# Weight chunks queued ahead of attention loads, a three-step path for the first block's weights, and six offsets for an operand pair

## Chip, cores and metric

The kernel runs on one NeuronCore of one Trainium2 chip. The metric is the device time of one execution in microseconds (us), the median of repeated runs. Engines are named as the profile names them: PE is TensorE, PEld its weight loads, DVE is VectorE, ACT is ScalarE, POOL is GpSimd, SP is SyncE, whose queue issues all of this kernel's DMAs.

## The reference, cut to what matters

Three stages run in a row over 4608 tokens of width 512.

```
# attention in chunks of 64, 8 batches x 8 heads x 576 x 64 (q, k, v are float32)
scores = q_c @ k_c.T / sqrt(64);  attn = softmax(scores);  x = attn @ v_c
x = x.transpose(0, 2, 1, 3).reshape(4608, 512)
# first MoE: w_in 512 x 2048, w_out 2048 x 512 (float64)
h = x @ w_in
g = h * clip(h + 3, 0, 6) / 6
x = g @ w_out
# second MoE: w_in 512 x 1024, w_out 1024 x 512 (float64), g_ln
h = x @ w_in
solu = h * softmax(h)
out = layernorm(solu) * g_ln @ w_out
```

The weights are float64 in device memory, so every chunk of them is converted to float32 on the core before it is used.

## The kernel before, in words

**Stages.** 36 attention units of 128 tokens make 9 blocks of 512 tokens. The first MoE runs block by block; the attention units of the next block are computed inside the current block, in `slot(b, f)`. Each block loops over 16 chunks `f` of the hidden width. Per chunk, `moe_h` (L267) does 12 matmuls with the stationary chunk `wi[f]`, and `moe_o` (L292) does 12 with `wo[f]`. Twelve, because each operand is split into a high and a low part and three of the four products are kept. `moe_o` is called one chunk late: PE's order is h(f), out(f-1), h(f+1), out(f). The second MoE takes 36 tiles of 128 tokens: `h2(t)`, 24 matmuls with the stationary operand `x_hi`/`x_lo`, and three tiles later `out_t`, 24 matmuls with the stationary operand `l_hi`/`l_lo` and the moving operand `wi`.

**A weight chunk's way in the first block.** `fetch` (L127) brings 512 KB of float64 words by an SP DMA. `rescale` (L139) is one ACT pass over the high words. `convert` (L144) is DVE work into an int32 tile `s` (4 buffers in rotation): one AND (L152) and two shift-or operations (L157) per chunk. With two chunks in one call the order is AND, AND and then four shift-ors, alternating. `split_w` (L170) takes the next chunk from the queue `ready`: an ACT cast to the high part (L73) and a POOL subtraction for the low part (L74), both reading `s`. Chunks of `w_in` are called i0 to i15 here, those of `w_out` o0 to o15.

**The activation's way.** After h(f): ACT relu into `t` (L278), DVE product with the clip (L282), ACT cast to `g_hi` (L73), and in the first and the last block a POOL subtraction to `g_lo` (L74).

**Order.** The schedule is manual: each engine executes its instructions in the order in which the code issues them, and waits in that order. In the first block, an iteration f of the code issues h(f) with its relu, one split (chunk i f+2), the activation's three steps, `convert` of o f and i f+3, out(f-1), the attention slot, rescales for o f+1 and i f+4, and one split (chunk o f). The slot puts eight small exponentials per unit on ACT where f is a multiple of 4 (L214), and a normalising product on DVE (L228).

**Buffers.** Tiles lie one behind the other in their pools. All tiles allocated ahead of the second MoE's pools have a length that is a multiple of 512 bytes, apart from a few small ones at the very start, so that `x_hi`, `x_lo`, `g_hi`, `g_lo`, `wi` and `wo` all begin at the same place within 512 bytes. The second MoE's pool `b2` begins there too; it holds ten [128, 1] tiles of 32 bytes each among its large ones, and pool `b3` with `l_hi` and `l_lo` (three buffers each) comes behind it. So `l_hi` and `l_lo` begin 320 bytes further within 512 bytes than `wi`.

**PSUM.** `ps_att`, `ps_h` have two banks each, `ps_acc` four, for the sums of `moe_o`. Ahead of the first block the attention units 0 to 3 use banks of `ps_att` and `ps_h`.

Of the kernel before, what the change touches and what calls it, by code (L numbers as in the profile page):

```python
# [8 lines left out]
F32 = mybir.dt.float32  # L9
F32R = mybir.dt.float32r  # L10
# [6 lines left out]
P = 128  # L17
# [4 lines left out]
def tile_kernel(  # L22
# [59 lines left out]
    def wo_slot(f, dtype):  # L82
        return wap.tile([P, 2, DM], dtype, tag=f"wo{f}", name=f"wo{f}")
# [43 lines left out]
    def fetch(kind, f):  # L127
        src = {"i": w_in, "o": w_out, "2": w_in2}[kind]
        if kind == "2" and f >= KD * NS:
            src = w_out2[f - KD * NS]  # L130
        else:
            src = src[f]
        raw = SLOTS[kind](f, F32).rearrange("p w n -> p (w n)").rearrange("p (n w) -> p n w", w=2)
        raws[kind, f] = raw
        nc.sync.dma_start(
            out=raw.bitcast(I32), in_=src.bitcast(I32).rearrange("p (n w) -> p n w", w=2)
        )

    def rescale(*key):  # L139
        if key in raws:  # L140
            r = raws[key][:, :, 1]
            nc.scalar.activation(out=r, in_=r, func=AF.Copy, scale=2.0**-112)  # L142
# [48 lines left out]
    def attn_scores(u, ps=att_psum, pt=None):  # L191
        scv = scores(u, ps)
        mx = ap2.tile([P, H], F32, tag="mx", name="mx")
        nc.vector.tensor_reduce(out=mx, in_=scv, axis=AX.X, op=ALU.max)
        pt = att_tile(ap2, "p") if pt is None else pt
        nc.vector.tensor_sub(
            out=pt, in0=scv, in1=mx[:, :, None].to_broadcast([P, H, D])
        )
        nc.scalar.activation(out=pt, in_=pt, func=AF.Exp, scale=0.125)
        p_t[u] = pt  # L200
# [111 lines left out]
                nc.sync.dma_start(out=x2d[b, :, dc], in_=xo)  # L312


    kbs, qps, vs = [kbd], [], []
    for i in range(3):
        kbs.append(wo_slot(NF - 1 - i, F32).rearrange("p c (h k) -> p c h k", h=H))
    for i in range(3, 6):
        qps.append(wo_slot(NF - 1 - i, F32).rearrange("p c (h k) -> p c h k", h=H))
    vs = wo_slot(NF - 7, F32).rearrange("p c (h k) -> p c h k", h=H)  # L320

    load_qk(0)
    load_qk(1, qps[0][:, 0], diagonal(kbs[1], nc.gpsimd))
# [5 lines left out]
    fetch("i", 1)  # L329
    load_v(2, vs[:, 0])  # L330
    load_v(3, vs[:, 1])
    fetch("o", 0)
    fetch("i", 2)
    fetch("o", 1)
    nc.sync.dma_start(out=g_sb, in_=g_ln)
    make_identity(nc, ident)
    diagonal(pbd, nc.gpsimd)
    nc.gpsimd.memset(three, 3.0)
    xs = new_x()
    attn_scores(0)  # L340
    attn_scores(1)
    load_qk(4)
    attn_norm(0, nc.gpsimd)
    attn_scores(2, h_psum, qps[0][:, 1])
    attn_transpose(0, pbd, h_psum)
    rescale("i", 0)
    attn_norm(1)
    attn_scores(3, h_psum, qps[1][:, 1])
    attn_transpose(1, kbs[1])
    attn_norm(2)  # L350
    attn_pv(0, pbd, *xs)
    load_v(4)
    attn_transpose(2, kbs[2], h_psum)
    attn_norm(3)
    convert(("i", 0))
    attn_pv(1, kbs[1], *xs)
    load_v(5)
    rescale("i", 1)
    attn_transpose(3, kbs[3], h_psum)
    split_w(1)  # L360
    attn_pv(2, kbs[2], *xs)
    convert(("i", 1))
    attn_pv(3, kbs[3], *xs)
    rescale("i", 2)
    split_w(1)
    attn_scores_act(4)
    load_qk(5)
    for f in range(2, NF):
        if f < NF - 7:
            fetch("o", f)  # L370
        if f + 1 < NF:
            fetch("i", f + 1)
    for f in range(NF - 7, NF):
        fetch("o", f)
    convert(("i", 2))
    rescale("o", 0)
    rescale("i", 3)
    x2, xr2 = {}, {}

    def fetch_x2(c):  # L380
# [47 lines left out]
    for b in range(NB):  # L428
        first, last = b == 0, b == NB - 1
        if not last:  # L430
            xn[b + 1] = new_x()
        for f in range(NF):
            h = moe_h(f, *xn[b])
            if first:
                split_w(1)
            pend.append((b, f, moe_g(*h, nc.gpsimd if first or last else nc.vector)))
            if f % 4 == 3:
                slot(b, f)
            if first:
                convert(("o", f), ("i", f + 3))  # L440
            if len(pend) > 1:
                moe_o(*pend.pop(0))
            if f % 4 != 3:
                slot(b, f)
            if first:
                rescale("o", f + 1)
                rescale("i", f + 4)
            split_w(1 if first else 2)
            if last:
                fetch("2", f)  # L450
                rescale("2", f - 1)
# [13 lines left out]


    b2 = ctx.enter_context(tc.tile_pool(name="b2", bufs=2, reuse_waits="tile"))
    b3 = ctx.enter_context(tc.tile_pool(name="b3", bufs=3, reuse_waits="tile"))
    ps_2 = ctx.enter_context(tc.tile_pool(name="ps_2", bufs=3, space=PSUM, reuse_waits="tile"))
    ps_o = ctx.enter_context(tc.tile_pool(name="ps_o", bufs=2, space=PSUM, reuse_waits="tile"))  # L470

# [2 lines left out]
    def h2(t):  # L474
        x_hi, x_lo = x2[t // UPB]
        o = (t % UPB) * P
        hp = ps_2.tile([P, FF2], F32, tag="h2", name="hp2")
        for s in range(NS):
            n = 0
            for kk in range(KD):  # L480
                for a, w in ((x_hi, 0), (x_hi, 1), (x_lo, 0)):
                    nc.tensor.matmul(  # L482
                        hp[:, s * DM : (s + 1) * DM], a[:, kk, o : o + P], wi[kk * NS + s][:, w],
                        start=(n == 0), stop=(n == 3 * KD - 1),
                    )
                    n += 1
        nmx = b2.tile([P, 1], F32, tag="nmx", name="nmx")
        nc.vector.tensor_reduce(out=nmx, in_=hp, axis=AX.X, op=ALU.max, negate=True)  # L488
        e = b2.tile([P, FF2], F32, tag="e", name="e")
        r = b2.tile([P, 1], F32, tag="r", name="r")  # L490
        nc.scalar.activation(out=e, in_=hp, func=AF.Exp, bias=nmx, accum_out=r)  # L491
        nc.vector.tensor_scalar_add(out=r, in0=r, scalar1=1e-9)
        nc.vector.reciprocal(out=r, in_=r)
        mu = b2.tile([P, 1], F32, tag="mu", name="mu")
        nc.vector.scalar_tensor_tensor(
            out=e, in0=e, scalar=r, in1=hp, op0=ALU.mult, op1=ALU.mult, accum_out=mu
        )
        nc.vector.tensor_scalar_mul(out=mu, in0=mu, scalar1=1.0 / FF2)
        d = b2.tile([P, FF2], F32, tag="d", name="d")
        nc.vector.tensor_scalar_sub(out=d, in0=e, scalar1=mu)  # L500
        d_t[t] = d
# [16 lines left out]
    def chain_square(t):  # L518
        d = d_t.pop(t)
        junk = b2.tile([P, FF2], F32, tag="junk", name="junk", bufs=1)  # L520
        va = b2.tile([P, 1], F32, tag="va", name="va")
        nc.scalar.activation(out=junk, in_=d, func=AF.Square, accum_out=va)
        va_t[t] = va

    def chain_rstd(t):
        va = va_t.pop(t)
        nc.vector.tensor_scalar(
            out=va, in0=va, scalar1=1.0 / FF2, scalar2=1e-6, op0=ALU.mult, op1=ALU.add
        )
        y = b3.tile([P, 1], F32, tag="y", name="y", bufs=4)  # L530
        yi = y.bitcast(I32)
        nc.vector.tensor_single_scalar(
            out=yi, in_=va.bitcast(I32), scalar=1, op=ALU.logical_shift_right
        )
        nc.vector.tensor_scalar(
            out=yi, in0=yi, scalar1=-1.0, scalar2=float(RSQRT_SEED), op0=ALU.mult, op1=ALU.add
        )
        tt = b2.tile([P, 1], F32, tag="tt", name="tt")
        for _ in range(3):
            nc.gpsimd.tensor_mul(out=tt, in0=y, in1=y)  # L540
            nc.gpsimd.tensor_mul(out=tt, in0=tt, in1=va)
            nc.gpsimd.tensor_scalar(
                out=tt, in0=tt, scalar1=-0.5, scalar2=1.5, op0=ALU.mult, op1=ALU.add
            )
            nc.gpsimd.tensor_mul(out=y, in0=y, in1=tt)
        rs_t[t] = y

    def split_l(t):
        turn_moves(t, (0, 1), nc.scalar.copy)
        m = m_t.pop(t)[0].rearrange("p a (f j) -> p f a j", j=32)  # L550
        l_hi = b3.tile([P, NF2, P], F32R, tag="l_hi", name="l_hi")
        l_lo = b3.tile([P, NF2, P], F32R, tag="l_lo", name="l_lo")
        hv, lv = [l.rearrange("p f (a j) -> p f a j", j=32) for l in (l_hi, l_lo)]
        split(hv, lv, m, nc.gpsimd)
        l_t[t] = (l_hi, l_lo)
# [90 lines left out]
```

## Time and profile before

| | us |
|---|---|
| median of 3 runs | 1311.71 (1311.7 to 1312.77) |
| the profiled execution, its own time | 1311.98 |
| the profiled execution, span from first to last instruction | 1310.0 |
| PE busy in the span | 1277.4 (98%) |
| PEld, DVE, ACT, POOL busy | 1041.7, 794.0, 581.8, 298.5 |
| chain that ended last: PE 89%, issue 3%, POOL 3%, DVE 2% | |

The page gives each engine's busy time, the chain of work that ended last, and the costliest groups of instructions. A matmul record is longer than the distance to the next one, since matmuls overlap, so rates are read from the distance between starts. A stretch is given in us from the start of the span.

### The profile page before, as it was taken

Reading aid. Unit: us, or ns where it says so; the run is one execution under the profiler, and the core shown is the slowest. Engines: PE = TensorE matmul, PEld = TensorE weight load, DVE = VectorE, ACT = ScalarE, POOL = GpSimd, SP = SyncE. Lnnn points to the kernel's source line nnn. Section 1 sums busy time; section 2 is a strip of 40 time slices with the busy share of each in tenths; the row PEclk is TensorE's granted clock in tenths of the full one; section 3 lists DMA queues with packets and bytes.
Section 4 is the critical chain, followed back from the end, with each engine's and each line's share of the span. In section 5 each row is a group of like instructions: output and inputs, shape, how many; then the busy total and the mean of one; then the engine's idle time right before and its main releaser. Section 6 shows DMA issues by size and latency. Waiting matters only on the chain.

```text
span 1310.0 us, 17877 instructions
## 1 busy us (share of the span) xinstructions
PE 1277.4 (98%) x6368; PEld 1041.7 (80%) x6368; DVE 794.0 (61%) x1556; ACT 581.8 (44%) x1106; POOL 298.5 (23%) x562
## 2 busy tenths in 40 slices
PE   6699999999999999999999999999999999999998
PEld 5566788888888888888888888888888888888887
DVE  6788655655655655656555555469766555555542
ACT  4566422222322222222322222445687666666665
POOL 2465200000000000000000000355355444444444
PEclk9899999999999999999999999999999999999999
DMA  7910110110110210200200200444132221222111
GB/s 236 409 62 25 57 49 25 57 49 25 58 47 25 77 29 25 81 25 25 81 25 28 78 25 1 129 129 129 28 94 82 80 81 49 81 81 73 57 49 57
DMA packets 52649, 92.41 MB, mean 71 GB/s; under 512 B 9552, under 2 KB 18768, under 8 KB 52560
## 3 DMA queue, kind: packets, MB, share of 16 engines
q1 hardware_dynamic: 52560, 91.27, 21.8%
q8 instruction: 50, 0.82, 0.2%
q14 instruction: 39, 0.32, 0.1%
HBM read 62.92 MB, written 18.87 MB: 62 GB/s over the span
## 4 chain that ended last, share of the span: by engine, by line
PE 89%; issue 3%; POOL 3%; DVE 2%; DMA 1%; ACT 1%; SPq 1%; POOLq 0%; ACTq 0%; DVEq 0%
PE acc L298 27%; PE hp L272 26%; PE po L564 15%; PE hp L482 15%; PE att L261 2%; PE att L186 2%; POOL g_lo L74 1%; POOL wo L74 1%; DMA wi<-in_moe_w_in 1%; DVE s L157 1%; POOL wi L74 1%; DVE s L152 1%; SPq L112 0%; DVE x_lo L74 0%; DVE t L282 0%
## 5 line engine op out<-in xcount | busy, mean ns | idle before, releaser
L298 PE MATMUL acc<-g_hi,wo 128*128 128x512 f32 x1152 | 295.0, 397 | 16.1 <-ACT wo L73 14.2
L272 PE MATMUL hp<-x_hi,wi 128*128 128x512 f32 x1152 | 285.1, 390 | 0.0
L298 PEld LDWEIGHTS acc<-g_hi,wo 128*128 128x128 f32 x1152 | 213.1, 189 | 73.1 <-ACT wo L73 18.9
L278 ACT ACTIVATE t<-hp,three 128x512 f32<-128x512 f32 x144 | 99.0, 687 | 372.6 <-PE hp L272 372.2
L272 PEld LDWEIGHTS hp<-x_hi,wi 128*128 128x128 f32 x1152 | 215.9, 188 | 44.9 <-ACT wi L142 0.2
L282 DVE SCALAR_TENSOR_TENSOR t<-t,hp 128x512 f32<-128x512 f32 x144 | 99.1, 688 | 234.4 <-ACT t L278 234.4
L74 POOL TENSOR_TENSOR g_lo<-t,g_hi 128x512 fp32r<-128x512 f32 x32 | 45.8, 1431 | 715.1 <-PE acc L298 672.5
L482 PE MATMUL hp<-wi,x_hi 128*128 128x512 f32 x576 | 177.8, 390 | 0.0
L298 PE MATMUL acc<-g_lo,wo 128*128 128x512 f32 x576 | 154.4, 390 | 0.0
L272 PE MATMUL hp<-x_lo,wi 128*128 128x512 f32 x576 | 153.9, 389 | 0.0
L564 PE MATMUL po<-wi,l_hi 128*128 128x512 f32 x576 | 140.2, 396 | 0.0
L251 DVE STREAM_TRANSPOSE pbd<-p 32x128 f32<-32x128 f32 x448 | 135.3, 302 | 5.7
L73 ACT CAST g_hi<-t 128x512 fp32r<-128x512 f32 x144 | 89.3, 620 | 107.9 <-DVE t L282 107.9
L564 PEld LDWEIGHTS po<-wi,l_hi 128*128 128x128 f32 x576 | 108.3, 188 | 25.6
L482 PEld LDWEIGHTS hp<-wi,x_hi 128*128 128x128 f32 x576 | 108.2, 188 | 23.5
L298 PEld LDWEIGHTS acc<-g_lo,wo 128*128 128x128 f32 x576 | 108.6, 189 | 22.9
L74 POOL TENSOR_TENSOR l_lo<-m,l_hi 128x1024 fp32r<-128x1024 f32 x36 | 86.6, 2406 | 174.1 <-ACT l_hi L73 152.0
L272 PEld LDWEIGHTS hp<-x_lo,wi 128*128 128x128 f32 x576 | 108.1, 188 | 22.5
L74 DVE TENSOR_TENSOR g_lo<-t,g_hi 128x512 fp32r<-128x512 f32 x112 | 77.6, 693 | 76.8 <-ACT g_hi L73 76.8
L516 ACT COPY m<-tr 32x256 f32<-32x256 f32 x288 | 115.8, 402 | 2.9
L482 PE MATMUL hp<-wi,x_lo 128*128 128x512 f32 x288 | 112.4, 390 | 0.0
L491 ACT ACTIVATE e<-hp,nmx 128x1024 f32<-128x1024 f32 x36 | 40.2, 1116 | 111.3 <-DVE nmx L488 111.3
(91 smaller groups left out, 1299.7 us busy)
## 6 DMA issues: line engine op xcount, KB each, us to landing
wi<-in_moe_w_in SPq DMA_DIRECT2D x24, 512.0 KB, 7.3
x2d<-xo SPq DMA_DIRECT2D x36, 256.0 KB, 2.8
xo<-x2d SPq DMA_DIRECT2D x36, 256.0 KB, 4.3
m<-tr SPq DMA_DIRECT2D x288, 32.0 KB, 1.8
out<-ob SPq DMA_DIRECT2D x36, 256.0 KB, 2.2
v<-in_v SPq DMA_DIRECT2D x34, 256.0 KB, 2.6
q<-in_q SPq DMA_DIRECT2D x33, 256.0 KB, 3.5
kbd<-in_k SPq DMA_DIRECT2D x66, 128.0 KB, 3.5
```

Source lines behind the costliest of these rows:

```text
L73: nc.scalar.copy(out=hi, in_=src)
L74: (eng or nc.vector).tensor_sub(out=lo, in0=src, in1=hi.bitcast(F32))
L186: nc.tensor.matmul(sc[r0 : r0 + D, h // 2], qt[:, h], kt[:, :, h], start=True, stop=True)
L251: nc.vector.transpose(out=pb[o : o + 32, s // 2, c, s % 2], in_=pv[s * 32 : s * 32 + 32, c, e],)
L272: nc.tensor.matmul(hp, wi[f][:, a, kk * P : (kk + 1) * P], b[:, kk], start=(n == 0), stop=(n == 3 * KD - 1),)
L278: nc.scalar.activation(out=t, in_=hp, func=AF.Relu, bias=three[:])
L282: nc.vector.scalar_tensor_tensor(out=t, in0=t, scalar=6.0, in1=hp, op0=ALU.min, op1=ALU.mult)
L298: nc.tensor.matmul(acc[dc], wo[f][:, w, dc * P : (dc + 1) * P], g[i], start=(f == 0 and n == 0), stop=(f == NF - 1 and n == 2),)
L482: nc.tensor.matmul(hp[:, s * DM : (s + 1) * DM], a[:, kk, o : o + P], wi[kk * NS + s][:, w], start=(n == 0), stop=(n == 3 * KD - 1),)
L491: nc.scalar.activation(out=e, in_=hp, func=AF.Exp, bias=nmx, accum_out=r)
L516: move(out=m[b * 32 : b * 32 + 32, a], in_=tr[a * 32 : a * 32 + 32, b])
L564: nc.tensor.matmul(po, a[:, f], wi[KD * NS + f][:, w], start=(n == 0), stop=(n == 3 * NF2 - 1),)
```

## The change

- **Fetch order.** i2, i3, i4 and o2 are fetched earlier, ahead of the loads of unit 4 or right behind them, and i5, o3, i6, o4 ahead of the load of unit 5, which waits for the scores of unit 4. In the rest, `fetch("i", f + 2)` stands ahead of `fetch("o", f)`. The small load of `g_ln` moves behind unit 5's.
- **Attention units 0 to 3** write their scores into the four accumulator banks, their transposes into `ps_att`, and their products into `ps_h`. The conversion of i0 is issued ahead of the normalisation of unit 2.
- **First block.** `convert` is issued ahead of the activation's steps, and for o f+1 instead of o f (i f+3 as before). An iteration has two splits as before: the first is now chunk o f (issued between `convert` and the activation's steps), the second is i f+2 (issued behind the slot). Rescales are for o f+2 and i f+4. So a chunk is converted in one iteration, split in the next and used by PE in a later one.
- **Second MoE.** The small tiles move into a pool `bs` behind `b3`. Each of the three buffers of `l_hi` and `l_lo` becomes a tile of its own, 512 bytes longer than its contents, which begin 0, 16 and 64 elements (`l_hi`) or 8, 32 and 112 elements (`l_lo`) behind the tile's start.

```diff
+    def acc_psum(i):
+        return lambda: ps_acc.tile([P, DM], F32, tag=f"acc{i}", name=f"acc{i}")
...
     load_v(3, vs[:, 1])
+    fetch("i", 2)
     fetch("o", 0)
-    fetch("i", 2)
+    fetch("i", 3)
     fetch("o", 1)
-    nc.sync.dma_start(out=g_sb, in_=g_ln)
...
-    attn_scores(0)
-    attn_scores(1)
+    attn_scores(0, acc_psum(0))
+    attn_scores(1, acc_psum(1))
     load_qk(4)
+    fetch("i", 4)
+    fetch("o", 2)
     attn_norm(0, nc.gpsimd)
-    attn_scores(2, h_psum, qps[0][:, 1])
-    attn_transpose(0, pbd, h_psum)
+    attn_scores(2, acc_psum(2), qps[0][:, 1])
+    attn_transpose(0, pbd)
     rescale("i", 0)
     attn_norm(1)
-    attn_scores(3, h_psum, qps[1][:, 1])
+    attn_scores(3, acc_psum(3), qps[1][:, 1])
     attn_transpose(1, kbs[1])
+    convert(("i", 0))
     attn_norm(2)
-    attn_pv(0, pbd, *xs)
+    attn_pv(0, pbd, *xs, h_psum)
+    attn_transpose(2, kbs[2])
+    rescale("i", 1)
+    attn_norm(3)
+    attn_pv(1, kbs[1], *xs, h_psum)
+    split_w(1)
     load_v(4)
-    attn_transpose(2, kbs[2], h_psum)
-    attn_norm(3)
-    convert(("i", 0))
-    attn_pv(1, kbs[1], *xs)
     load_v(5)
-    rescale("i", 1)
-    attn_transpose(3, kbs[3], h_psum)
-    split_w(1)
-    attn_pv(2, kbs[2], *xs)
+    fetch("i", 5)
+    fetch("o", 3)
+    fetch("i", 6)
+    fetch("o", 4)
+    attn_transpose(3, kbs[3])
     convert(("i", 1))
-    attn_pv(3, kbs[3], *xs)
+    attn_pv(2, kbs[2], *xs, h_psum)
     rescale("i", 2)
+    attn_pv(3, kbs[3], *xs, h_psum)
     split_w(1)
     attn_scores_act(4)
     load_qk(5)
...
-    convert(("i", 2))
     rescale("o", 0)
+    convert(("i", 2), ("o", 0))
     rescale("i", 3)
+    rescale("o", 1)
...
             h = moe_h(f, *xn[b])
             if first:
+                convert(("o", f + 1), ("i", f + 3))
                 split_w(1)
             pend.append((b, f, moe_g(*h, nc.gpsimd if first or last else nc.vector)))
             if f % 4 == 3:
                 slot(b, f)
-            if first:
-                convert(("o", f), ("i", f + 3))
             if len(pend) > 1:
                 moe_o(*pend.pop(0))
             if f % 4 != 3:
                 slot(b, f)
             if first:
-                rescale("o", f + 1)
+                split_w(1)
+                rescale("o", f + 2)
                 rescale("i", f + 4)
-            split_w(1 if first else 2)
+            else:
+                split_w(2)
...
-    b3 = ctx.enter_context(tc.tile_pool(name="b3", bufs=3, reuse_waits="tile"))
+    b3 = ctx.enter_context(tc.tile_pool(name="b3", bufs=1, reuse_waits="tile"))
+    bs = ctx.enter_context(tc.tile_pool(name="bs", bufs=2, reuse_waits="tile"))
...
+    L_AT = {"l_hi": (0, 16, 64), "l_lo": (8, 32, 112)}
+
+    def l_tile(name, i):
+        o = L_AT[name][i]
+        l = b3.tile([P, FF2 + P], F32R, tag=f"{name}{i}", name=f"{name}{i}")
+        return l[:, o : o + FF2].rearrange("p (f t) -> p f t", t=P)
...
-        l_hi = b3.tile([P, NF2, P], F32R, tag="l_hi", name="l_hi")
-        l_lo = b3.tile([P, NF2, P], F32R, tag="l_lo", name="l_lo")
+        l_hi, l_lo = l_tile("l_hi", t % 3), l_tile("l_lo", t % 3)
```

## Rows read from the trace of the kernel before

**Rows 1.** Busy time by stretch: PE, PEld, DVE, ACT, POOL, PEclk, DMA share, GB/s.

```profile
25.00:30.00 5.00, 4.31 (x42) 3.55 (x43) 4.07 (x8) 3.38 (x6) 1.97 (x2) 1.00 0.15 55
30.00:43.00 13.00, 3.54 (x16) 2.61 (x14) 8.29 (x12) 6.38 (x24) 3.27 (x3) 0.78 0.98 373
43.00:152.00 109.00, 102.38 (x515) 77.87 (x516) 87.04 (x122) 64.35 (x147) 59.77 (x44) 0.98 0.32 118
```

**Rows 2.** PE's waits from 28 to 152 us: total us, times, longest.

```profile
PE acc L298 <- ACT wo L73: 14.2, 7, 9.6
```

**Rows 3.** Timeline of PE, first block: the start of out(0), out(1), out(12), out(15).

```profile
43.12 3.78 PE L298 MATMUL acc<-g_hi,wo 128*128 128x512 f32 x8 [9.58 <-ACT wo L73]
...
50.70 1.19 PE L298 MATMUL acc<-g_hi,wo 128*128 128x512 f32 x4
...
128.97 1.20 PE L298 MATMUL acc<-g_hi,wo 128*128 128x512 f32 x4 [0.73 <-ACT wo L73]
...
149.54 1.98 PE L298 MATMUL acc<-g_hi,wo 128*128 128x512 f32 x8
```

**Rows 4.** Timeline of POOL in one iteration of the first block.

```profile
65.12 1.29 POOL L74 TENSOR_TENSOR wo<-s,wo 128x512 fp32r<-128x512 f32 x1 [3.50 <-ACT wo L73]
66.36 1.29 POOL L74 TENSOR_TENSOR wi<-s,wi 128x512 fp32r<-128x512 f32 x1
67.61 1.48 POOL L74 TENSOR_TENSOR g_lo<-t,g_hi 128x512 fp32r<-128x512 f32 x1
```

**Rows 5.** Timeline of DVE at the same place.

```profile
61.76 0.43 DVE L152 TENSOR_SCALAR s<-wo 128x512 int32<-128x512 int32 x1
62.10 0.42 DVE L152 TENSOR_SCALAR s<-wi 128x512 int32<-128x512 int32 x1
...
65.79 0.69 DVE L282 SCALAR_TENSOR_TENSOR t<-t,hp 128x512 f32<-128x512 f32 x1 [0.86 <-ACT t L278]
66.40 1.54 DVE L152 TENSOR_SCALAR s<-wo 128x512 int32<-128x512 int32 x1
67.86 1.52 DVE L152 TENSOR_SCALAR s<-wi 128x512 int32<-128x512 int32 x1
69.29 0.68 DVE L157 SCALAR_TENSOR_TENSOR s<-wo,s 128x512 int32<-128x512 int32 x1
69.90 0.68 DVE L157 SCALAR_TENSOR_TENSOR s<-wi,s 128x512 int32<-128x512 int32 x1
```

**Rows 6.** Timeline of all engines: a POOL operation issued between DVE's.

```profile
46.31 1.58 POOL L74 TENSOR_TENSOR g_lo<-t,g_hi 128x512 fp32r<-128x512 f32 x1 [0.18 <-ACT g_hi L73]
46.33 0.41 DVE L152 TENSOR_SCALAR s<-wi 128x512 int32<-128x512 int32 x1
46.66 1.77 DVE L157 SCALAR_TENSOR_TENSOR s<-wo,s 128x512 int32<-128x512 int32 x1
```

**Rows 7.** Timeline of ACT: a rescale, and one slot's eight exponentials, first and behind.

```profile
35.80 0.65 ACT L142 ACTIVATE wi<-wi 128x512 f32<-128x512 f32 x1 [5.99 <-DMA wi<-in_moe_w_in]
...
95.04 0.62 ACT L73 CAST g_hi<-t 128x512 fp32r<-128x512 f32 x1 [0.25 <-DVE t L282]
95.56 0.31 ACT L214 ACTIVATE p<-att,mx 128x64 f32<-128x64 f32 x1
...
97.89 0.72 ACT L142 ACTIVATE wo<-wo 128x512 f32<-128x512 f32 x1
```

**Rows 8.** Timeline of PE, a later block: 24 matmuls stand between these starts.

```profile
317.43 1.98 PE L298 MATMUL acc<-g_hi,wo 128*128 128x512 f32 x8
...
322.87 1.98 PE L298 MATMUL acc<-g_hi,wo 128*128 128x512 f32 x8
```

**Rows 9.** Timeline of PE, second MoE: 24 matmuls of `out_t`, then 24 of `h2`.

```profile
1106.48 3.90 PE L564 MATMUL po<-wi,l_hi 128*128 128x512 f32 x16
...
1112.08 0.62 PE L482 MATMUL hp<-wi,x_hi 128*128 128x512 f32 x2
...
1117.55 3.90 PE L564 MATMUL po<-wi,l_hi 128*128 128x512 f32 x16
```

More of the change, by code (lines that the diff above doesn't have):

```diff
@@ L312, in moe_o @@
                 nc.sync.dma_start(out=x2d[b, :, dc], in_=xo)
-    kbs, qps, vs = [kbd], [], []
+    kbs, qps = [kbd], []
     for i in range(3):
@@ L367, in tile_kernel @@
     load_qk(5)
[L368 to L372, printed above, removed]
+    nc.sync.dma_start(out=g_sb, in_=g_ln)
+    for f in range(5, NF - 7):
+        fetch("i", f + 2)
+        fetch("o", f)
     for f in range(NF - 7, NF):
+        if f + 2 < NF:
+            fetch("i", f + 2)
         fetch("o", f)
-    convert(("i", 2))
     rescale("o", 0)
+    convert(("i", 2), ("o", 0))
     rescale("i", 3)
+    rescale("o", 1)
     x2, xr2 = {}, {}
@@ L486, in h2 @@
                     n += 1
-        nmx = b2.tile([P, 1], F32, tag="nmx", name="nmx")
+        nmx = bs.tile([P, 1], F32, tag="nmx", name="nmx")
         nc.vector.tensor_reduce(out=nmx, in_=hp, axis=AX.X, op=ALU.max, negate=True)
         e = b2.tile([P, FF2], F32, tag="e", name="e")
-        r = b2.tile([P, 1], F32, tag="r", name="r")
+        r = bs.tile([P, 1], F32, tag="r", name="r")
         nc.scalar.activation(out=e, in_=hp, func=AF.Exp, bias=nmx, accum_out=r)
@@ L493, in h2 @@
         nc.vector.reciprocal(out=r, in_=r)
-        mu = b2.tile([P, 1], F32, tag="mu", name="mu")
+        mu = bs.tile([P, 1], F32, tag="mu", name="mu")
         nc.vector.scalar_tensor_tensor(
@@ L520, in chain_square @@
         junk = b2.tile([P, FF2], F32, tag="junk", name="junk", bufs=1)
-        va = b2.tile([P, 1], F32, tag="va", name="va")
+        va = bs.tile([P, 1], F32, tag="va", name="va")
         nc.scalar.activation(out=junk, in_=d, func=AF.Square, accum_out=va)
@@ L529, in chain_rstd @@
         )
-        y = b3.tile([P, 1], F32, tag="y", name="y", bufs=4)
+        y = bs.tile([P, 1], F32, tag="y", name="y", bufs=4)
         yi = y.bitcast(I32)
@@ L537, in chain_rstd @@
         )
-        tt = b2.tile([P, 1], F32, tag="tt", name="tt")
+        tt = bs.tile([P, 1], F32, tag="tt", name="tt")
         for _ in range(3):
```

## The prediction

> **What bounds the kernel now.** I read the busy times by stretch first, then PE's waits, then the timelines of single engines. Behind 152 us PE has no wait worth a term, so the loss sits ahead of that. There the stretches show three things. From 25 to 30 us the DMA engines are nearly idle (share 0.15): SP's queue stands at the load of unit 5. From 30 to 43 us PE is busy 3.5 of 13 us. From 43 to 152 us PE looks busy, but POOL and DVE together take 59.8 + 87.0 of 109 us [rows 1]. PE's only large wait there is for the casts of `wo`, 14.2 us, 9.6 of them ahead of out(0) [rows 2, 3]. The reader should see how out(0) comes to be late: o0 is converted in one call with i3, and i3's rescale waits for its DMA until 35.80 [rows 7].
>
> From out(1) to out(12) the block takes (128.97 - 50.70) / 11 = 7.12 us an iteration [rows 3]. PE's own need is 5.44 us for 24 matmuls [rows 8]. What fills the rest? A free AND takes 0.42 us; with a POOL subtraction running it takes 1.52, and it ends 0.3 us behind POOL [rows 4, 5]. So a conversion and a POOL subtraction exclude each other. POOL gets in between two DVE instructions that follow without a gap: issued at 46.31, it runs behind the AND that ends at 46.74, until 47.89 (1.15 us), and the shift-or issued at 46.66 ends only at 48.43 [rows 6]. The product with the clip, which reads PSUM, isn't held: 0.69 us with POOL busy. One iteration holds six conversions (to the start of what follows: 2 x 0.34 + 4 x 0.60 = 3.08 us) and three subtractions (1.25 apart). Before, the three subtractions run one behind the other from 65.12 to 69.09, while relu, product and `g_hi` are made beside them, and then the shift-ors run. Exclusive work stands nearly without a gap, and that is the 7.12.
>
> **The change part by part.**
>
> *Fetch order.* The DMA gap goes, and i3 is there before its rescale is due. PE gains only what no other wait takes over, so I price it inside the start-up below.
>
> *Start-up.* The conversion of i0 (0.42 + 2 x 0.7 = 1.8 us) moves ahead of unit 2's normalisation on DVE, in the attention chain; part of it fills a DVE gap, so h(0) starts about 1 us later, near 28.8. The extra banks free scores, transposes and products of each other, but the chain runs through DVE and ACT, so I price them at nothing; the DVE work above hides them, and without that cover they could be worth what h(0) loses, 1 us. Then DVE does i2 with o0 from about 30.2 to 33.3, and o1 with i3 behind it, with i2's subtraction in between: to 37.5. Only then comes the product of chunk 0, because `convert` is now issued ahead of it. `g_hi` is ready at 38.8, eight exponentials follow on ACT (95.56 to 97.89: 2.3 us [rows 7]), and o0's cast, which now stands behind the slot, ends near 41.8. So out(0) starts at 41.8 instead of 43.12. The stall that i3's DMA caused goes to DVE and ACT: 1.3 us gained, not 9.6. The unit's product and o0's subtraction then put the AND of i4 at 43.85.
>
> *Three steps.* PE and ACT no longer wait for a conversion of the same iteration. But a new ring closes. `convert` in iteration f takes two `s` tiles. With four in rotation, i f+3 takes that of i f+1, which POOL reads in the second split of iteration f-1. POOL does that behind `g_lo` of f-1, which needs the product of f-1, which stands on DVE behind the conversion of f-1. Before, i f+3 took the tile of i f+1 as well, but POOL had split that ahead of `g_lo` of f-1. Round the ring, from the AND of i f+3: 0.34 + 4 x 0.60 to the start of the product; o f's subtraction gets in between, 1.15 (rows 6); product 0.69, `g_hi` 0.62, `g_lo` 1.25, subtraction of i f+2 1.25, and 0.25 that I allow for three hand-overs. Sum: 7.95 us, against 7.12. During product and `g_hi` neither side has exclusive work, and that 1.3 us is the loss.
>
> The slot adds to the ring, since the second split now stands behind it on ACT. At f = 4, 8, 12 the exponentials hold i f+2's cast for 2.3 us, of which `g_lo` hides little, and unit product and subtraction exclude each other: +2.25. At f = 2, 6, 10 two copies of 0.58 each: +0.5. At f = 3, 7, 11 one cast and the unit's DVE work: +0.25. Out(1) can start when `g_hi` of 1 is ready: 43.85 + 0.34 + 2.40 + 1.15 + 0.69 + 0.62 = 49.1 (50.70 before). Eleven iterations later: 49.1 + 11 x 7.95 + 3 x 0.5 + 3 x 0.25 + 2 x 2.25 = 143.3 for out(12), where it was 128.97. The last two conversions have no `w_in` partner (three operations, 1.0 us less): 7.95 - 1.0 + 2.25 = 9.2 and 6.9 us, to 159.4 for out(14); behind it h and one more round put out(15) at 165 instead of 149.54. From there PE sets the pace as before. Part: +15.5 us.
>
> Bounds. If o f's subtraction fell into the gap of 1.3 us, the ring would be 6.8 us and the part about +2.5; rows 6 speak for the other place. If a second AND or the rescales fell into the ring (0.34 each), +20.
>
> *Six offsets.* In the first MoE 24 matmuls take 5.44 us, 226.6 ns each [rows 8]; in `out_t` (1112.08 - 1106.48) / 24 = 233.3; in `h2` 5.47 us in all [rows 9]. The first two differ in where the stationary operand lies against the moving one: at the same place within 512 bytes, and 320 bytes off. After, the six tiles lie 0, 64, 256 (`l_hi`) and 32, 128, 448 bytes (`l_lo`) off. If the place is the cause, the tile at 0 gains 12 x 16 x 6.7 ns = 1.3 us for certain; all six would gain 864 x 6.7 ns = 5.8, and `h2` 1.0 more. Nothing in the trace says what the other five do; as a bound they cost as much again as 320 bytes does, 672 x 6.7 ns = 4.5, less the 1.3. I take -3.0, ends -6.8 and +3.2: the tile at 0 and about a third of the rest. The Trainium skill speaks against any gain (SBUF — State Buffer, "Who interferes with whom"): TensorE has two read ports of its own, one for moving data and one for weights, and never waits on anyone. By that rule the offsets are worth nothing and the sum is 1327.5; the trace, with 233.3 against 226.6 ns for the same shape, doesn't fit that the place is indifferent, though it doesn't prove it.
>
> *Nothing else.* Moving the small tiles changes no operation; blocks 1 to 8 keep their order, as the `else` branch is the old one.
>
> Sum against the profiled execution, 1311.98 (2 us over its span, 0.3 over the median of the runs): + 15.5 - 3.0 = 1324.5; I say 1324.
>
> **Rivals.** *The ring doesn't bind* (faster). Place: the AND of i f+3. If its `s` tile is free before `g_lo` of f-1 has run, DVE converts beside the activation chain. Then only the exclusive work counts, 2.74 + 3 x 1.15 = 6.2 us an iteration, more than PE's 5.44: out(15) near 41.8 + 15 x 6.2 + 2 = 137, -12.5, with the offsets 1296.5. It decides where that AND starts: within 2 us of the product before it, or behind i f+1's subtraction. For it speaks that PE's 14.2 us of waits are for the very casts that move [rows 2]; against it the order of POOL's queue. Chance 0.13.
>
> *POOL's o split in the gap*: ring 6.8, block +2.5, in all 1311.5, no change. Chance 0.13.
>
> *PE's clock falls.* PE would be idle some 2.5 us in each ring and 5 at the slots with exponentials; from 30 to 43 us the granted clock was 0.78 on average, and out(0)'s first eight matmuls took 3.78 us against 1.98 later [rows 1, 3]. If that spread, PE would need 5.44 x 3.78 / 1.98 = 10.4 us a ring at the lower level (1.2 GHz): over four or five rings some 11 us more, 1335. Against it: in the block before, with 1.7 us an iteration beyond the 24 matmuls, 0.98 was granted. Chance 0.06.
>
> **How the numbers follow.** The forecast has 0.68: its own range, from the ring's bounds and those of the offsets, is 1315 to 1333. The range that should hold 8 of 10 reaches down to the rival without change: 1307 to 1333. A run of this kernel can tell 0.2% (2.6 us). Faster: 0.13 and a quarter of the third case, 0.16. Same: half of that, 0.07. Slower: 0.77.
>
> **What the profile after would show.** Right: out(0) near 42, out(1) near 49; from there starts of out(f) about 8 us apart and 10 behind each slot with exponentials; the AND of i f+3 starting just behind POOL's `wi` subtraction; DVE idle for over 1 us behind each product; out(15) near 165; PE waiting for `g_hi` or `g_lo`, not for `wo`. `out_t` at 226.6 ns for tiles t with t mod 3 = 0 at least. Wrong: starts of out(f) under 7 us apart, or an AND that runs beside `g_hi`; or `out_t` at 233 throughout.

## The result and the profile after

The changed kernel takes 1324.7 us (median of 4 runs, 1324.05 to 1325.35), the kernel before 1312.2 beside it. The ratio is 1.0095 (95% interval 1.0078 to 1.0113): slower by 0.95%. The span of the profiled execution grew by 12.5 us, from 1310.0 to 1322.5.

The stretches of [rows 1], in the same columns, with the last one reaching to the end of the slow part:

```profile
25.00:30.00 5.00, 4.35 (x53) 3.97 (x54) 4.92 (x7) 4.55 (x10) 2.29 (x2) 0.88 1.03 398
30.00:43.00 13.00, 7.01 (x26) 5.18 (x25) 9.84 (x20) 7.62 (x26) 7.41 (x5) 0.88 1.04 367
43.00:168.00 125.00, 103.98 (x512) 82.17 (x511) 83.03 (x115) 60.73 (x143) 59.72 (x43) 0.93 0.24 86
```

The fetch order did its part: from 25 to 30 us the DMA share is 1.03 instead of 0.15, and from 30 to 43 us PE is busy 7.01 us instead of 3.5. The loss is in the last row: 512 PE instructions are spread over 125 us. Here is what PE waited for in the first block (line, total, times, longest), beside [rows 2], without two waits of 0.6 us:

```profile
PE acc L298 <- ACT g_hi L73: 13.2, 6, 3.3
PE att L261 <- ACT pbd L239: 7.2, 4, 2.9
PE acc L298 <- ACT wo L73: 6.0, 1, 6.0
```

Before, the waits were for `wo`. Now out(f) finds its weight chunk late once, at out(0), and from then on the activation is late (`g_hi`), and with it the attention slot. The starts of some out(f) on PE, beside [rows 3]:

```profile
40.64 3.88 PE L298 MATMUL acc<-g_hi,wo 128*128 128x512 f32 x8 [5.99 <-ACT wo L73]
49.06 1.98 PE L298 MATMUL acc<-g_hi,wo 128*128 128x512 f32 x8
...
141.84 3.49 PE L298 MATMUL acc<-g_hi,wo 128*128 128x512 f32 x8 [2.39 <-ACT g_hi L73]
...
159.81 2.11 PE L298 MATMUL acc<-g_hi,wo 128*128 128x512 f32 x8
165.38 1.98 PE L298 MATMUL acc<-g_hi,wo 128*128 128x512 f32 x8
```

Out(0) gains 2.5 us (43.12 before), out(1) 1.6, and then eleven iterations take 92.78 us instead of 78.27. Out(15) starts 15.8 us late. One round of the ring on DVE, from one product with the clip (L282) to the next, stands like this (compare [rows 5]; a bracket is idle time ahead of the instruction, with its releaser):

```profile
115.86 0.68 DVE L282 SCALAR_TENSOR_TENSOR t<-t,hp 128x512 f32<-128x512 f32 x1
118.37 0.53 DVE L152 TENSOR_SCALAR s<-wo 128x512 int32<-128x512 int32 x1 [1.84 <-issue]
120.07 1.48 DVE L152 TENSOR_SCALAR s<-wi 128x512 int32<-128x512 int32 x1 [1.18 <-POOL wi L74]
121.48 0.68 DVE L157 SCALAR_TENSOR_TENSOR s<-wo,s 128x512 int32<-128x512 int32 x1
...
123.88 0.67 DVE L282 SCALAR_TENSOR_TENSOR t<-t,hp 128x512 f32<-128x512 f32 x1
```

POOL in the same round (compare [rows 4]):

```profile
117.31 1.30 POOL L74 TENSOR_TENSOR g_lo<-t,g_hi 128x512 fp32r<-128x512 f32 x1 [3.74 <-issue]
118.57 1.47 POOL L74 TENSOR_TENSOR wi<-s,wi 128x512 fp32r<-128x512 f32 x1
120.00 1.27 POOL L74 TENSOR_TENSOR wo<-s,wo 128x512 fp32r<-128x512 f32 x1
```

And ACT, whose prices of before are in [rows 7]:

```profile
116.57 0.62 ACT L73 CAST g_hi<-t 128x512 fp32r<-128x512 f32 x1 [4.35 <-DVE t L282]
117.61 0.67 ACT L142 ACTIVATE wo<-wo 128x512 f32<-128x512 f32 x1
```

Read the three together: product at 115.86, `g_hi` at 116.57, `g_lo` at 117.31, POOL's subtraction of `wi` from 118.57 to 120.04, the AND of the next `w_in` chunk at 120.07, four shift-ors, next product at 123.88. DVE stands idle for 3 us of the 8.02, and POOL for some 4 (3.74 ahead of 117.31). The first AND has its own wait: it starts at 118.37, just behind the rescale of its chunk, which ACT ends at 118.28. That is a second ring, beside the one that I had seen.

Rounds of this kind stand behind chunks 1, 5 and 9. Over the block these are DVE's waits, 43 to 150 us (total, times, longest):

```profile
DVE sm L226 <- ACT p L214: 9.2, 3, 3.1
DVE s L152 <- POOL g_lo L74: 9.1, 3, 3.1
DVE s L152 <- issue: 5.5, 3, 1.8
DVE s L152 <- POOL wi L74: 3.5, 3, 1.2
DVE x_lo L74 <- ACT x_hi L73: 3.5, 3, 1.2
```

The wait for the `s` tile, which the prediction named, is the one put down to `POOL wi`: 3.5 of 30.8 us. The second and the third line are waits for a rescale. In the round behind chunk 2, `g_lo` ends at 57.18, the rescale at 58.10, and the AND starts at 58.19; in e2 below the same wait is put down to ACT's rescale. The first and the last are waits for the slot's work on ACT, the exponentials and `x_hi`.

In the second MoE, `out_t` of three tiles in a row, beside [rows 9]:

```profile
945.44 3.80 PE L584 MATMUL po<-wi,l_hi 128*128 128x512 f32 x16
949.07 2.02 PE L584 MATMUL po<-wi,l_lo 128*128 128x512 f32 x8
...
956.38 3.89 PE L584 MATMUL po<-wi,l_hi 128*128 128x512 f32 x16
960.11 2.02 PE L584 MATMUL po<-wi,l_lo 128*128 128x512 f32 x8
...
967.41 3.79 PE L584 MATMUL po<-wi,l_hi 128*128 128x512 f32 x16
971.04 2.00 PE L584 MATMUL po<-wi,l_lo 128*128 128x512 f32 x8
972.87 0.62 PE L496 MATMUL hp<-wi,x_hi 128*128 128x512 f32 x2
```

From the starts, per matmul: `l_hi` at 0 bytes 3.63 / 16 = 227 ns, at 64 bytes 233, at 256 bytes 227; `l_lo` at 448 bytes 1.83 / 8 = 229. Over all tiles of the two traces, three take 16.545 us where they took 16.795, so the 36 save 3.0 us, and `h2` 0.6 more. Together with the block: 15.84 - 3.6 = +12.2 of the +12.5.

### The profile page after: what moved, and what is told of

Its sections match the earlier page's. It is cut to its first block, busy times and chain, and to the rows that moved or that the text cites. A ratio compares the mean times of both kernels' runs of the same rounds, so it can differ in the third digit from the quotient of the medians.

```text
span 1322.5 us, 17863 instructions
## 1 busy us (share of the span) xinstructions
PE 1279.6 (97%) x6368; PEld 1049.5 (79%) x6368; DVE 792.4 (60%) x1556; ACT 579.4 (44%) x1106; POOL 303.3 (23%) x562
## 4 chain that ended last, share of the span: by engine, by line
PE 86%; DVE 1%; issue 0%; ACT 0%; ACTq 0%; DVEq 0%
PE acc L298 26%; PE hp L272 26%; PE po L584 15%; PE hp L496 15%; PE att L261 2%; PE att L186 2%; DVE s L157 1%; DVE t L282 0%; DVE x_lo L74 0%; DVE s L152 0%; DVE s L163 0%; ACT g_hi L73 0%; ACT t L278 0%; ACT ob L590 0%; ACT pbd L239 0%
## 5 line engine op out<-in xcount | busy, mean ns | idle before, releaser
L282 DVE SCALAR_TENSOR_TENSOR t<-t,hp 128x512 f32<-128x512 f32 x144 | 99.1, 688 | 220.6 <-ACT t L278 220.6
L298 PEld LDWEIGHTS acc<-g_lo,wo 128*128 128x128 f32 x576 | 110.2, 191 | 23.5
L584 PEld LDWEIGHTS po<-wi,l_hi 128*128 128x128 f32 x576 | 108.3, 188 | 23.5
```

The lines of the kernel that those rows point to most:

```text
L282: nc.vector.scalar_tensor_tensor(out=t, in0=t, scalar=6.0, in1=hp, op0=ALU.min, op1=ALU.mult)
L298: nc.tensor.matmul(acc[dc], wo[f][:, w, dc * P : (dc + 1) * P], g[i], start=(f == 0 and n == 0), stop=(f == NF - 1 and n == 2),)
L584: nc.tensor.matmul(po, a[:, f], wi[KD * NS + f][:, w], start=(n == 0), stop=(n == 3 * NF2 - 1),)
```

## The experiments

The question was whether the loss is the ring, as worked out ahead, and which link of it; what the fetch order is worth by itself; and whether the offsets act by their place. All times are medians; "before" is the kernel before, run beside them (1311.4, 1312.0 and 1312.1 us in three batches). The block is compared by the starts of out(f) in the traces:

| kernel | us | ratio to before (95%) | out(0) | out(1) | out(12) | out(15) | us per iteration, 1 to 12 |
|---|---|---|---|---|---|---|---|
| before | 1312 | | 43.12 | 50.70 | 128.97 | 149.54 | 7.12 |
| after | 1324.7 | 1.0095 (1.0078-1.0113) | 40.64 | 49.06 | 141.84 | 165.38 | 8.43 |
| e12: conversion ahead, in before | 1335.1 | 1.0175 (1.0158-1.0192) | 45.97 | 53.82 | 151.13 | 172.48 | 8.85 |
| e6: conversion behind, in after | 1301.15 | 0.9916 (0.9901-0.9931) | 37.49 | 45.13 | 120.49 | 141.80 | 6.85 |
| e2: eight `s` buffers | 1323.66 | 1.0095 (1.0080-1.0110) | 40.61 | 48.81 | 141.04 | 164.58 | 8.38 |
| e3: both splits ahead | 1325.51 | 1.0107 (1.0092-1.0122) | 37.38 | 47.44 | 142.92 | 164.59 | 8.68 |
| e7: rescale an iteration earlier | 1321.7 | 1.0073 (1.0052-1.0093) | 40.34 | 48.42 | 140.54 | 162.79 | 8.37 |
| e5: e2 and e7 together | 1313.12 | 1.0006 (0.9997-1.0016) | 40.93 | 49.03 | 132.47 | 156.30 | 7.59 |
| e10: e6, e2, e7, zero offsets | 1297.84 | 0.9892 (0.9877-0.9907) | 37.73 | 44.89 | 120.25 | 141.60 | 6.85 |
| e9: e6, zero offsets | 1297.81 | 0.9891 (0.9876-0.9906) | 37.83 | 45.48 | 120.82 | 142.12 | 6.85 |
| e4: fetch order alone | 1307.34 | 0.9969 (0.9958-0.9980) | 38.41 | 45.99 | 124.25 | 144.85 | 7.11 |

### The link in the ring: more buffers, or an earlier split

In the after kernel, e2 gives `s` eight buffers (the late tag `xo` shares them); e3 does both splits ahead of the activation.

```
e2:
-wcp = ctx.enter_context(tc.tile_pool(name="wcp", bufs=4))
+wcp = ctx.enter_context(tc.tile_pool(name="wcp", bufs=8))
-    return wcp.tile([P, BT], F32, tag="xo", name="xo")
+    return wcp.tile([P, BT], F32, tag="s", name="xo")
e3:
                 convert(("o", f + 1), ("i", f + 3))
-                split_w(1)
+                split_w(2)
...
             if first:
-                split_w(1)
                 rescale("o", f + 2)
```

> The changed kernel with the s tiles and the output stages in one rotation of eight buffers instead of two of four, in the same memory. Theory ring: i f+3 no longer takes the tile of i f+1, the AND doesn't wait for the subtraction behind g_lo, and an iteration falls from about 8.7 us to the exclusive work, 6.2 to 7 us: out(15) at 137 to 150 us instead of 165.4, 1296 to 1309 us. Rival (exclusive work alone, or PE's waits for the attention copies, sets the pace and the tile's wait is covered): out(15) stays within 3 us of 165, 1322 to 1327 us.

> The changed kernel with both splits of an iteration issued ahead of the activation's steps, four s tiles as before. POOL then subtracts i f+2 ahead of g_lo, so the tile comes free without waiting for the product. Theory ring: broken here too, without a byte of memory: an iteration takes the two conversions and three subtractions, about 6.2 to 7 us, out(15) at 140 to 150 us, 1299 to 1309 us. Rival (tile's wait covered): 1322 us or more.

Both theories fell: 1323.66 and 1325.51 us, within the noise of after. With them falls the theory that the `s` tile alone closes the ring. The trace of e2 on DVE shows what stands in its place:

```profile
115.31 0.68 DVE L282 SCALAR_TENSOR_TENSOR t<-t,hp 128x512 f32<-128x512 f32 x1
117.75 0.53 DVE L152 TENSOR_SCALAR s<-wo 128x512 int32<-128x512 int32 x1 [1.77 <-ACT wo L142]
118.38 1.34 DVE L152 TENSOR_SCALAR s<-wi 128x512 int32<-128x512 int32 x1
119.64 1.76 DVE L157 SCALAR_TENSOR_TENSOR s<-wo,s 128x512 int32<-128x512 int32 x1
...
123.13 0.67 DVE L282 SCALAR_TENSOR_TENSOR t<-t,hp 128x512 f32<-128x512 f32 x1
```

The second AND no longer waits for its tile. But the first one waits 1.77 us for the rescale, which ACT executes behind `g_hi`, which needs the product ahead of it. By then POOL's subtractions are in line, and they get in between the conversions instead (1.34 and 1.76 us where 0.41 and 0.68 are free). The round is 7.82 us. In e3 the first AND waits in the same way (1.32 us in the round that starts at 116.41, 2.53 in the next), and the rounds from product to product take 7.9, 8.7, 8.55 and 10.0 us in turn. Out(0) starts 3.3 us earlier than in after and out(12) 1.1 later, so DVE's rounds set the pace, not PE's start.

### Both links, and the rescale alone

e7 moves the rescales one iteration ahead, with four `s` buffers; e5 adds the eight buffers.

```
     rescale("o", 1)
+    rescale("i", 4)
+    rescale("o", 2)
...
-                rescale("o", f + 2)
-                rescale("i", f + 4)
+                rescale("o", f + 3)
+                rescale("i", f + 5)
```

> The changed kernel with every rescale one iteration earlier, four s tiles as changed. Theory two rings, each enough by itself: the tile's ring stays closed, iterations near 8 us, out(15) at 162 to 167 us, 1321 to 1326 us. Rival (the rescale was the ring all along, the tile's wait is covered): out(15) at 150 us or earlier, below 1312 us.

> The changed kernel with eight tiles in rotation (as in the second run) and every rescale issued one iteration earlier. The second run left an iteration at its length, and its trace shows DVE's AND waiting for ACT's rescale, which stands behind g_hi on ACT just as the tile's subtraction stands behind g_lo on POOL. Theory two rings, each enough by itself: with both open an iteration falls to the exclusive work, 6.5 to 7.1 us, out(15) at 140 to 150 us instead of 165.4, 1299 to 1310 us. Rival (the exclusive work with its gaps sets 8 us whatever waits): 1321 us or more.

Against after, e2 gained 1.0 us, which is within the noise, and e7 3.0, of which 1.3 behind out(12). Both together gained 11.6 us (1313.12), so either link by itself keeps most of the loss up. That is how two rings with a common part, product to `g_hi`, behave. In e5 DVE has no wait for tile or rescale from 43 to 150 us; the rounds behind chunks 1, 5 and 9 fall from 8.03 to 3.67 us, those behind 2, 6 and 10 rise from 8.45 to 9.66, and the others stay. But e5 fell short of its range. Its remaining loss is where the slot has exponentials: 10.06 us a round, where e6 below takes 6.91. DVE in such an iteration:

```profile
99.60 0.68 DVE L282 SCALAR_TENSOR_TENSOR t<-t,hp 128x512 f32<-128x512 f32 x1
103.34 0.17 DVE L226 TENSOR_SCALAR sm<-sm 128x8 f32<-128x8 f32 x1 [3.06 <-ACT p L214]
```

The unit's sum waits 3.06 us for ACT's exponentials, and on DVE the next conversion is queued behind it. With the conversion issued ahead of the product, nothing is left on DVE to do in that time. Out(8) to out(9) takes 10.06 us there as in after (10.07).

### Undo the position of `convert`, or do it alone

e6 is the after kernel with `convert` moved back behind `moe_g`; all else (fetch order, chunk o f+1, splits, rescales, offsets) stays. e12 is the other way about: the kernel before with only that line moved ahead.

```
e6 (in after):
             if first:
-                convert(("o", f + 1), ("i", f + 3))
                 split_w(1)
             pend.append((b, f, moe_g(*h, nc.gpsimd if first or last else nc.vector)))
+            if first:
+                convert(("o", f + 1), ("i", f + 3))
e12 (in before):
             if first:
+                convert(("o", f), ("i", f + 3))
                 split_w(1)
             pend.append((b, f, moe_g(*h, nc.gpsimd if first or last else nc.vector)))
...
-            if first:
-                convert(("o", f), ("i", f + 3))
```

> The changed kernel with convert issued behind the activation's steps again, everything else as changed. Both rings then close over two iterations instead of one, since the product of an iteration no longer stands behind its conversion on DVE. Theory rings: out(0) near 38 us, 6.7 to 7.1 us an iteration, out(15) at 140 to 147 us, 1299 to 1307 us. Rival (what costs is that o f is split beside the conversion, or PE's falling clock): out(15) at 155 us or later, 1315 us or more.

> The kernel before with one thing moved: convert of o f and i f+3 issued ahead of the activation's steps instead of behind them; fetches, splits, rescales and offsets as before. Theory order on DVE: this line alone makes the loss. The rescale ring closes (rescale behind g_hi on ACT, product behind the conversion on DVE): product and g_hi 1.34, rescales 1.2, the rest of the exclusive work 5.5, about 8 us an iteration instead of 7.1, and 2.3 more where ACT has the exponentials first: out(15) at 160 to 167 us instead of 149.5, 1320 to 1329 us. Rival (the three-step path as a whole, with its later splits, makes the loss, not this line): within 3 us of 1312.

e6 takes 1301.15 us, 23.5 less than after and 10.9 less than before. e12 takes 1335.1, 23.0 more than before. So the position of one call is worth 23 us in either kernel, and it is all of the loss. The rest of the change gains the 10.9 us: the offsets 3.6, the fetch order 4.7 at out(15) (e4), and what makes up the remaining 2.6 no run takes apart. DVE in a round of e6:

```profile
97.82 0.68 DVE L282 SCALAR_TENSOR_TENSOR t<-t,hp 128x512 f32<-128x512 f32 x1
98.42 0.92 DVE L152 TENSOR_SCALAR s<-wo 128x512 int32<-128x512 int32 x1
...
99.59 1.79 DVE L157 SCALAR_TENSOR_TENSOR s<-wo,s 128x512 int32<-128x512 int32 x1
101.31 1.77 DVE L157 SCALAR_TENSOR_TENSOR s<-wi,s 128x512 int32<-128x512 int32 x1
...
104.21 0.67 DVE L282 SCALAR_TENSOR_TENSOR t<-t,hp 128x512 f32<-128x512 f32 x1
```

The conversion starts right behind the product and runs while ACT makes `g_hi`. POOL gets in three times, and DVE has no gap: 6.4 us a round. DVE is busy 98 of 107 us in this kernel from 43 to 150 us, against 75 in after; a record that POOL holds up counts as busy.

e12's direction was right, its size was off: 22.9 us were lost up to out(15), where 10 to 17 had been expected. DVE shows where. The AND of i3 waits 3.57 us for its rescale, since i3's DMA is late in the old fetch order, and the product of chunk 0 now stands behind that: it starts at 40.62 instead of 37.05. The round behind it takes 10.04 us instead of 7.85. Then the rounds take 7.9, 8.75, 8.55 and 10.05 in turn, where about 8 had been expected for all but the last kind: 95.7 us for eleven, against 77.9. PE waits 26.7 us for casts of `wo` here, as out(f) needs o f, converted in the same iteration and cast behind the slot. No product up to chunk 12 waits for PE's h(f) or its relu, though, so these waits follow DVE's pace and don't make it.

### The fetch order alone

e4 is the kernel before with the new order of `fetch` calls and `g_ln`'s load, nothing else.

```
+    fetch("i", 2)
     fetch("o", 0)
-    fetch("i", 2)
+    fetch("i", 3)
     fetch("o", 1)
...
     load_qk(4)
+    fetch("i", 4)
+    fetch("o", 2)
...
     load_v(5)
+    fetch("i", 5)
+    fetch("o", 3)
+    fetch("i", 6)
+    fetch("o", 4)
```

> The kernel before with only the new order of fetches. i3 lands before its rescale is due, so ACT no longer stands from 30 to 35.8 us. Theory of the start-up sum: the stall goes on to DVE and ACT, out(0) comes at 37 to 38 us instead of 43.1, and from there the iterations keep their 7.1 us, so that 4 to 6 us stay: 1306 to 1308 us. Rival (the exclusive work is what counts, and it is not started earlier): out(15) within 2 us of 149.5, 1310 to 1312 us.

1307.34 us: out(0) starts 4.7 us earlier, and out(15) keeps all 4.7 (the whole run gains 4.1). So the fetch order is worth some 4.7 us where the conversion stands behind the product. In after, out(0) starts 2.5 us earlier, as o0's cast stands behind the product of chunk 0, which waits for two conversions, and behind the exponentials. (In iteration 0 the first split takes i2 and the second o0.)

### The place of `l_hi` and `l_lo`

e1 is the kernel before with the second MoE's code of after and all six tiles at zero. e8 adds a 64-byte tile to the constants ahead of everything, so that every operand moves by the same amount. e11 is e6 with other places: `l_hi` at 16, 192 and 384 bytes, `l_lo` at 256, 0 and 0. e9 is e6 with zeros. The places are worked out from the order and the lengths of the allocations; no view shows an address.

```
-    L_AT = {"l_hi": (0, 16, 64), "l_lo": (8, 32, 112)}
+    L_AT = {"l_hi": (0, 0, 0), "l_lo": (0, 0, 0)}       (e1, e8, e9, e10)
+    L_AT = {"l_hi": (4, 48, 96), "l_lo": (64, 0, 0)}    (e11)
+    const.tile([P, 16], F32, name="gap")                (e8)
```

> The kernel before with the second MoE of the changed one, but all six l tiles at offset 0, so that each lies at the same place within 512 bytes as wi. First block untouched. Theory place-against-the-moving-operand: every out_t takes 24 x 226.6 ns = 5.44 us instead of 5.60, and h2 behind it loses its slow first matmuls (5.44 instead of 5.47): 36 x 0.16 + 32 x 0.03 = 6.8 us less, 1305.4 us. Rival (each tile's rate hangs on something else that the six offsets changed along, such as one tile per buffer): no or partial gain, 1309 us or more.

> The first run's kernel (kernel before, l tiles at wi's place) with a gap of 64 bytes ahead of all large tiles, so that every operand of both MoEs begins 256 bytes past a multiple of 512 instead of 192. Theory place of the stationary operand against the moving one: nothing changes, 226.6 ns a matmul in out_t, 1305 us. Rival (the absolute place counts: 256 was slow for a tile of the changed kernel): out_t back at 231 to 233 ns, and other stages may slow down as well, 1309 us or more.

> The sixth run's kernel with other places of the l tiles against wi: 16, 192 and 384 bytes for l_hi, 256, 0 and 0 for l_lo. Theory that the place counts within 256 bytes: l_lo at 256 bytes as fast as at 0 (226.6 ns), l_hi at 384 as slow as l_lo was at 128 (232 ns), l_hi at 192 like l_lo at 448 (229 ns). Rival (within 512 bytes): 384 and 192 can be anything. For 16 bytes neither has a number.

> The sixth run's kernel (changed, convert behind the activation's steps) with all six l tiles at wi's place. The two gains add up if they are independent: 1301.2 less what the six mixed offsets leave, 36 x 5.44 against 12 x 16.55 for out_t (2.7 us) and 0.3 for h2: 1298.1 us.

> The kernel of the run before with eight tiles in rotation and every rescale one iteration earlier as well. Theory exclusive work: with convert behind the activation's steps neither ring binds any more, so opening them changes little: 1296 to 1299 us. Rival (the rings, over two iterations, still hold some iterations, those with exponentials above all): 1292 to 1295 us.

e1: 1305.18 us, ratio 0.9954 (0.9937 to 0.9971). `out_t` and `h2` each take 5.44 us a tile, at 226.6 ns a matmul:

```profile
1103.68 3.79 PE L571 MATMUL po<-wi,l_hi 128*128 128x512 f32 x16
1109.12 0.62 PE L483 MATMUL hp<-wi,x_hi 128*128 128x512 f32 x2
1114.56 3.79 PE L571 MATMUL po<-wi,l_hi 128*128 128x512 f32 x16
```

e8: 1305.67, ratio 0.9949 (0.9933 to 0.9964), the same 5.44. So the rate follows the place of the stationary operand against the moving one, not the address. e11 (one run, 1299.69 us), three tiles:

```profile
921.01 3.79 PE L584 MATMUL po<-wi,l_hi 128*128 128x512 f32 x16
924.64 1.98 PE L584 MATMUL po<-wi,l_lo 128*128 128x512 f32 x8
931.89 3.83 PE L584 MATMUL po<-wi,l_hi 128*128 128x512 f32 x16
935.56 1.99 PE L584 MATMUL po<-wi,l_lo 128*128 128x512 f32 x8
942.83 3.90 PE L584 MATMUL po<-wi,l_hi 128*128 128x512 f32 x16
946.56 2.02 PE L584 MATMUL po<-wi,l_lo 128*128 128x512 f32 x8
948.42 0.62 PE L496 MATMUL hp<-wi,x_hi 128*128 128x512 f32 x2
```

From `l_hi`'s start to `l_lo`'s: 3.63, 3.67 and 3.73 us for 16. With those of before and after this gives, in ns a matmul by bytes off: 0 and 256, 227; 16, 227; 192 and 448, 229; 32, 232.6; 64 and 320, 233; 128 and 384, 232.5 to 233.4. Four pairs of places 256 bytes apart agree within about a nanosecond; that of 128 bytes counts less, as its eight matmuls follow sixteen slow ones at 64.

One group doesn't fit. The third tile's `l_lo` lies at 0 and takes (948.42 - 946.56) / 8 = 232.5 ns a matmul, where the same tile takes 226 in e9, with `l_hi` at 0 too. It follows sixteen matmuls at 384 bytes. `h2` lost 0.03 us behind `out_t` in the kernel before, which points the same way: the first matmuls behind a slow stretch can be slow at a good place. How long that lasts wasn't settled.

e9 takes 1297.81 us, 14.3 less than before and faster than both kernels. e10 opens both links of the ring on top of it and takes 1297.84: with the conversion behind the product, tile and rescale don't bind.

## Why the prediction was right

**The ring.** Priced at 7.95 us, measured 8.02 in the round shown. Most links are as priced: AND with a subtraction behind it 1.41 (0.34 + 1.15 had been taken), four shift-ors 2.40, product 0.71 to the start of `g_hi`, `g_lo` 1.26. The subtraction of `wi` took 1.47 instead of 1.25; the first AND was still running when it was issued (118.37 to 118.90). The subtraction of o f did fall between the conversions and not into the gap, which rules out the rival at 1311.5. The AND of i f+3 started 4.2 us behind the product and 0.03 behind POOL's `wi`, which rules out the rival in which the ring doesn't bind (it was to start within 2 us). That rival's 6.2 us left out one of the two ANDs (2.74 instead of 3.08), so it should have read 6.5.

From product to product, DVE's rounds took 8.02 to 8.04 us behind chunks 1, 5 and 9 (7.95 forecast), 8.44 to 8.49 behind 2, 6 and 10 (8.45), 8.13 to 8.15 behind 3, 7 and 11 (8.2) and 10.06 to 10.09 behind 4 and 8 (10.2). The eleven make 94.0 us; 94.2 had been forecast.

**What the prediction missed in it.** It named one ring, closed by the `s` tile. There are two, and the second, through the rescale on ACT, is as long: 7.82 us in e2. The tile's wait shows only behind chunks 1, 5 and 9, 3.5 of DVE's 30.8 us. Behind 2, 6 and 10 DVE waits for the rescale, and where the slot has exponentials for these themselves, 3.06 us, as the unit's sum stands ahead of the conversion on DVE. What all these rounds share is that the next conversion hangs on work that ACT does behind `g_hi`; the sum had the parts of that path and their sizes. That the waits come out equally long, so that one ring's price fits rounds that another wait sets, is luck. The repair that the prediction's own words suggest, more buffers, gave 1.0 us, nothing clear of the noise. The bound of +20 "if the rescales fell into the ring" named the possibility without its mechanism.

**Start-up.** H(0) started at 28.94 (forecast 28.8) and out(0) at 40.64 (41.8). The difference is i2's subtraction: it was to get in between the conversions, but it was held until DVE was through with them, so the product of chunk 0 started at 36.38 and `g_hi` was ready at 37.71 instead of 38.8. POOL's record:

```profile
33.57 4.02 POOL L74 TENSOR_TENSOR wi<-s,wi 128x512 fp32r<-128x512 f32 x1 [3.29 <-ACT wi L73]
```

Out(1) at 49.06 (49.1) was hit by luck. It was to wait for `g_hi` of chunk 1, which was ready at 47.76; but PE was still at out(0) and h(2), 24 matmuls that took 8.42 us instead of 5.44, with a granted clock of 0.64. The extra banks for the first units, priced at nothing, were not run alone. That the gain moves to another wait is shown by out(0): 2.5 us earlier in after, 4.7 in e4, 5.6 in e6.

**The eleven iterations.** On PE they took 92.78 us, forecast 94.2; the late out(1) makes the difference. Their sum fitted, the pattern on PE didn't: starts of out(f) were to be some 8 us apart, and ten behind slots with exponentials. Ten was measured behind those of f = 4 and 8 (10.1), but also 5.6 us from out(2) to out(3), 6 to 7 and 10 to 11, and 9.8 to 12.3 before these. PE executes the unit's products at f = 3, 7, 11 ahead of out(f - 1), and they wait for ACT's copies, 7.2 us in all; this wait wasn't foreseen. It moves out(f) and costs little of its own, as DVE's rounds show. The last two steps were priced 9.2 and 6.9 us, and took 8.64 and 6.36 on DVE, but 18.0 on PE, where the unit's products come ahead of out(14). Out(12) had come 1.5 us early, so 159.4 and 165 met 159.81 and 165.38; that the two cancel is luck. Block: +15.84 against +15.5.

**The offsets.** Forecast -3.0, measured -3.6 with `h2` (3.0 of it in `out_t`). The sum was nearly right by a wrong distribution: the tile at 0 and "a third of the rest" had been taken, while the tile at 256 bytes gains all, that at 448 bytes 4 of 6.7 ns, and those at 32, 64 and 128 bytes less than one. The bound that the others could cost as much again was not met: the slowest place is no slower than that of before. By the rule of the Trainium skill (SBUF — State Buffer, "Who interferes with whom"), TensorE's ports for moving data and for weights are independent and it never waits on anyone, so nothing was to be gained. The measurement decides otherwise: the place alone took `out_t` from 5.60 to 5.44 us (e1), and moving all operands together changed nothing (e8).

**The clock.** The granted clock was 0.93 from 43 to 168 us (0.98 from 43 to 152 us before), and out(0) and out(12) ran eight matmuls in 3.88 and 3.49 us. The rival was to cost 11 us. In after no product from 43 to 150 us waits for PE's h(f) or its relu (DVE's waits above have no such line), and DVE's rounds behind chunks 5 and 9 take 8.04 and 8.02 us, though out(5) ran eight matmuls in 2.11 us and out(9) in 2.89. So slow matmuls fitted into time in which PE would have waited. No run held the clock by itself.

**The sum.** 1311.98 + 15.5 - 3.0 = 1324.5 forecast, 1324.7 measured.

## What to carry to other kernels

When work is moved ahead of a step on an in-order engine, follow every buffer and every producer of the moved work back to that step: here conversion, split and rescale all came back to the product, through two engines, and opening one of the two rings gave at most 3 us of the 23, both 11.6. A long independent call belongs behind the step that others wait for, where it fills the time of the hand-overs (98 of 107 us of DVE busy instead of 75). And stationary operands should lie at the same place within 256 bytes as the moving ones: in these runs that is up to 3% of each such matmul.

## What was not expected of the hardware

- The rate of a 128 x 512 fp32r matmul depends on the place of the stationary operand against the moving one, with a period of 256 bytes in the pairs measured: 226.6 ns at 0, 16 and 256, up to 233.4 elsewhere, and 232.5 at 0 right behind sixteen matmuls at 384. By what mechanism stays open.
- A POOL subtraction isn't always let in between two DVE instructions. In e5, POOL's `g_lo` was issued at 111.08 and has a record of 3.50 us, while DVE ran three shift-ors and a product without a gap:

```profile
111.54 0.68 DVE L157 SCALAR_TENSOR_TENSOR s<-wi,s 128x512 int32<-128x512 int32 x1
...
113.35 0.68 DVE L282 SCALAR_TENSOR_TENSOR t<-t,hp 128x512 f32<-128x512 f32 x1
```

```profile
111.08 3.50 POOL L74 TENSOR_TENSOR g_lo<-t,g_hi 128x512 fp32r<-128x512 f32 x1 [3.68 <-ACT g_hi L73]
```

  In the same kernel a subtraction of `wo` issued at 96.78 got in behind one instruction (the shift-or at 97.30 took 1.77 us). The 4.02 us of i2's subtraction in the start-up are of the first kind. Which of the two happens wasn't settled; the prediction's 1.15 us for each subtraction counts on the second.
